# Residue-major token order, crossbar transposes for the last four batches and half-array transposes for the first, in a fused attention and feed-forward kernel

## Chip, cores, metric

One core of one Trainium2 chip. The metric is device time in microseconds (us). A profiled execution gives a *span*, some 1.7 us shorter than the run's time, and the mean clock granted to the matrix engine. The engines are PE (matrix), DVE (vector), ACT (scalar), POOL (its queue issues the casting loads from memory) and SP (its queue issues the stores and, after the change, the crossbar transposes). Tiles are counted from 0, so the second tile is tile 1.

## The reference, cut

```python
# q, k, v: (8 batches, 8 heads, 576 tokens, 64), drawn as randn * 0.1
scores = q @ k.T / 8
mask_plain = (rel >= 0) & (rel < 32)                       # heads 0..3
mask_dil   = (rel >= 0) & (rel < 128) & (rel % 4 == 0)     # heads 4..7
attn = softmax(where(mask, scores, -1e9)); out = attn @ v  # x: (4608, 512)
h = relu(x @ w_in); y = (h * h) @ w_out                    # 512 -> 2048 -> 512
```

## The kernel before

Heads go in pairs `e`; pairs 0 and 1 are plain, 2 and 3 dilated. Tokens of a dilated head are wanted by residue modulo 4. For each batch and pair: q and k (`qb`, `kb`) are transposed on PE into PSUM (`pa`), copied into `qT` and, block-diagonally, into `kbd`; scores, exponential and mask give `pt`; value products (`po`) and the denominator (`pd`, a product with ones) give a piece of `xT`. The feed-forward runs in nine tiles of 512 tokens. Each tile has `G` = 32 slots of four matmuls of 512 columns, and batch b's attention steps are mixed into tile b-1 at given slots.

```python
def t_main(b, e, nm):                       # batches 0, 2..7 (cut)
    for hl in range(2):
        for jp in range(4):                 # 8 transposes of 72 columns for q or k of a pair
            nc.tensor.transpose(pv_[:, hl, 72*pos : 72*pos+72], rbs[b][nm][0:72, 2*e+hl, 128*jp : 128*jp+128], ident[0:72, 0:72])
    for hl in range(2):
        for jj in range(2):                 # 4 copies of 64 x 288, or 4 + 4 for k of a dilated pair
            ...
            elif nm == "q":                 # plain: every second element of qT (4 bytes apart)
                nc.scalar.copy(qT[rows, e, :].rearrange("p (u a j) -> p j u a", a=4, j=2)[:, jj], ...)

def t_part(b, e, nm, part):                 # batch 1, in two parts of tokens (cut)
            elif nm == "q":                 # plain: every fourth element (8 bytes apart)
                nc.scalar.copy(qT[rows, e, ...].rearrange("p (x c j) -> p j c x", c=2, j=2)[:, jj], src)

# denominators of half a dilated pair: three wide matmuls
dms = [(d3[:, :, 0:96], main[:, :, 0:96]), (d3[:, :, 64:M], main[:, :, 96:176]), (d3[:, :, 128:M], rem)]
# store of 128 output rows: one DMA
nc.sync.dma_start(out[tk0 + P*m : tk0 + P*m + P, :], osb[:, :])
```

The softmax here doesn't subtract the row's maximum and nothing guards it: scores larger than these inputs give would overflow.

Of the kernel before, what the change touches and what calls it, by code (L numbers as in the profile page):

```python
# [11 lines left out]
WIN = 32  # L12
RES = 4

ORDER = (0, 2, 1, 3)

FIRST = "q0 k0 q3 q2 k2 a0 k1 b0 q1 v2 o0 a1 a2 k3 b1 o1 b2 p0 o2 p2 a3 v3 b3 p1 o3 p3".split()
# [3 lines left out]
        "21:q1 23:k0 24:q2 25:k2 26:q0 27:v2 27:v3 27:a0 27:a2 28:k1 28:k3 29:o0 29:a1 29:Q1 29:q3 29:o2 "  # L21
        "29:o1 30:a3 30:Q0 31:K1 31:o3 32:K0 32:Q2 34:Q3 36:b0 37:b1 37:K2 37:K3 37:V2 39:p0 39:b2 39:V3 "
# [3 lines left out]
        "8:q0 10:k0 12:a0 12:b0 13:k1 13:q1 14:v2 14:v3 14:o0 16:q2 17:p0 17:a1 17:k2 19:b1 19:o1 21:a2 22:q3 "  # L26
        "24:b2 24:o2 25:k3 26:p1 26:a3 26:b3 27:p2 29:o3 31:p3"
# [4 lines left out]
def _masks() -> np.ndarray:  # L32





    j = np.arange(64)[:, None]
    c = np.arange(96)[None, :]
    band = ((c - j >= 0) & (c - j < WIN)).astype(np.float32)  # L40
    kr, km = j % RES, j // RES
    cc = np.arange(64)[None, :]
    qr, qm = cc // 16, cc % 16
    rem = ((kr == qr) & (qm - km >= 0)).astype(np.float32)
    one = np.concatenate([band, rem], axis=1)
    p = np.arange(128)
    ident = (p[:, None] == p[None, :]).astype(np.float32)
    ones = (p[:, None] // 64 == p[None, :] // 64).astype(np.float32)
    return np.concatenate([np.concatenate([one, one], axis=0), ident, ones], axis=1).astype(ml_dtypes.bfloat16)
# [3 lines left out]
def kernel(  # L53
# [9 lines left out]
    nc = tc.nc  # L63
# [13 lines left out]
    PT = 72  # L77
    JT = S // PT
    TA = 256
    NT = 512  # L80
    NTILES = NTOK // NT
    KT = DM // P
    NF = DFF // P
    MT = NT // P
    M = S // RES

    const = ctx.enter_context(tc.tile_pool(name="const", bufs=1))
    rb_pool = ctx.enter_context(tc.tile_pool(name="rb", bufs=2))
# [15 lines left out]
    mk = const.tile([P, 160 + 2 * P], bf16, name="mk")  # L104
    ident = mk[:, 160 : 160 + P]
    ones = mk[:, 160 + P : 160 + 2 * P]
    mask_p = const.tile([P, NB * 96], bf16, name="mask_p")
    mask_d = const.tile([P, 2 * 176 + 64], bf16, name="mask_d")
    mask_t = const.tile([P, 4 * 64 + 4 * 112 + 64], bf16, name="mask_t")
# [6 lines left out]
    xT = const.tile([P, KT, NTOK], bf16, name="xT")  # L116
    qT = const.tile([P, NE, S], bf16, name="qT")
# [6 lines left out]
    rbs, vds = {}, {}  # L124

    def load_qk(b: int, es):
        if b not in rbs:
            rbs[b] = {
                "q": rb_pool.tile([80, H, JT * D], bf16, name="qb"),
                "k": rb_pool.tile([80, H, JT * D], bf16, name="kb"),  # L130
            }
        for es_ in ([e for e in es if e < NE // 2], [e for e in es if e >= NE // 2]):
            if not es_:
                continue
            hs = slice(2 * es_[0], 2 * es_[-1] + 2)
            for nm, src in (("q", q), ("k", k)):
                if es_[0] < NE // 2:
                    nc.gpsimd.dma_start(  # L138
                        rbs[b][nm][0:PT, hs, :], src[b, hs, :, :].rearrange("h (p j) d -> p h (j d)", j=JT)
                    )  # L140
                else:
                    nc.gpsimd.dma_start(
                        rbs[b][nm][0:PT, hs, :].rearrange("p h (a x) -> p (h a) x", a=2),
                        src[b, hs, :, :].rearrange("h (a p r) d -> p (h a) (r d)", a=2, r=RES),
                    )

    def load_v(b: int, es):
        dst = vbd[b % 2]
        if b not in vds:
            vds[b] = vd_pool.tile([P, NE // 2, 2, RES * D], bf16, name="vd")  # L150
        for e in es:
            for hl in range(2):
                rows = slice(64 * hl, 64 * hl + 64)
                h = 2 * e + hl
                if e < NE // 2:
                    nc.gpsimd.dma_start(  # L156
                        dst[rows, e, :, rows], v[b, h].rearrange("(i p) d -> p i d", p=64)
                    )
                else:
                    nc.gpsimd.dma_start(  # L160
                        vds[b][rows, e - NE // 2, :, :],
                        v[b, h, 0:512, :].rearrange("(m p r) d -> p m (r d)", p=64, r=RES),
                    )
        if es[-1] == NE - 1:
# [7 lines left out]
    def load_part(b: int, part: int):  # L172

        t0, t1 = (0, TA) if part == 0 else (TA, S)
        if part == 0:
            rbs[b] = {
                "q": rb_pool.tile([80, H, JT * D], bf16, name="qb"),
                "k": rb_pool.tile([80, H, JT * D], bf16, name="kb"),
            }
            vds[b] = vd_pool.tile([P, NE // 2, 2, RES * D], bf16, name="vd")  # L180
        for nm, src in (("q", q), ("k", k)):
            nc.gpsimd.dma_start(
                rbs[b][nm][0 : (t1 - t0) // 4, :, 256 * part : 256 * part + 256],
                src[b, :, t0:t1, :].rearrange("h (p j) d -> p h (j d)", j=4),
            )
        dst = vbd[b % 2]
        for e in range(NE):
            for hl in range(2):
                rows = slice(64 * hl, 64 * hl + 64)
                h = 2 * e + hl  # L190
                if e < NE // 2:
                    nc.gpsimd.dma_start(
                        dst[rows, e, t0 // 64 : t1 // 64, rows],
                        v[b, h, t0:t1, :].rearrange("(i p) d -> p i d", p=64),
                    )
                else:
                    nc.gpsimd.dma_start(
                        vds[b][rows, e - NE // 2, part, :],
                        v[b, h, t0 : t0 + TA, :].rearrange("(p r) d -> p (r d)", r=RES),
                    )  # L200
        if part == 1:
            for hl in range(2):
                rows = slice(64 * hl, 64 * hl + 64)
                nc.gpsimd.dma_start(
                    dst[rows, NE // 2 : NE, 8, rows],
                    v[b, H // 2 + hl : H : 2, 512:S, :].rearrange("h p d -> p h d"),
                )

    def spread_part(b: int, e: int, part: int):
        for hl in range(2):  # L210
            rows = slice(64 * hl, 64 * hl + 64)
            nc.vector.tensor_copy(
                vbd[b % 2][rows, e, RES * part : RES * part + RES, rows],
                vds[b][rows, e - NE // 2, part, :].rearrange("p (r d) -> p r d", d=D),
            )

    def spread_v(b: int, e: int):

        for hl in range(2):
            rows = slice(64 * hl, 64 * hl + 64)  # L220
            nc.vector.tensor_copy(  # L221
                vbd[b % 2][rows, e, 0:8, rows],
                vds[b][rows, e - NE // 2, :, :].rearrange("p m (r d) -> p (m r) d", d=D),
            )


    def t_main(b: int, e: int, nm: str, pool=None, name="pa"):



        ps = (pool or ps_a).tile([P, 1024], bf16, name=name)
        dil = e >= NE // 2
        pv_ = ps[:, 0 : 2 * S // 2].rearrange("p (h x) -> p h x", h=2)
        for hl in range(2):
            for jp in range(JT // 2):
                pos = 2 * (jp % 2) + jp // 2 if dil else jp
                nc.tensor.transpose(  # L237
                    pv_[:, hl, PT * pos : PT * pos + PT], rbs[b][nm][0:PT, 2 * e + hl, P * jp : P * jp + P], ident[0:PT, 0:PT]
                )
        for hl in range(2):  # L240
            rows = slice(64 * hl, 64 * hl + 64)
            for jj in range(2):
                src = pv_[64 * jj : 64 * jj + 64, hl, :]
                if dil:
                    src = src.rearrange("p (c m) -> p c m", c=2)
                    if nm == "q":
                        nc.vector.tensor_copy(  # L247
                            qT[rows, e, :].rearrange("p (c j m) -> p c j m", c=2, j=2)[:, :, jj, :], src
                        )
                    else:  # L250
                        nc.vector.tensor_copy(
                            kbd[rows, e, 0:8, rows].rearrange("p (m c j) k -> p c j m k", c=2, j=2)[:, :, jj, :, :],
                            src[:, :, 0:128].rearrange("p c (m k) -> p c m k", m=2),
                        )
                        nc.vector.tensor_copy(
                            kbd[rows, e, 8, rows].rearrange("p (m c j) -> p c j m", c=2, j=2)[:, :, jj, :],
                            src[:, :, 128:M],
                        )
                elif nm == "q":
                    nc.scalar.copy(  # L260
# [423 lines left out]
```

## Time and profile before

| | before |
|---|---|
| time, median (3 runs) | 342.56 us (342.47 to 345.79) |
| span of the profiled run | 341.6 us |
| PE busy, matmuls | 315.0 us, 2508 |
| first feed-forward matmul starts at | 27.61 us |
| period of a tile mixed with attention, from tile 2 on | 34.65 us |
| a tile without attention | 27.7 us |

PE is the engine to watch. A stage in which it hardly waits (the mixed tiles from the third on) can only be shortened by fewer or shorter matmuls; a stage in which it waits (up to 78 us) by whatever it waits for. The prediction below shows the lines. It calls PE *cold* near the start of the program and *warm* later: in the kernel before, eight 72-column transposes take 0.46 us from start to start at 13.38 us and 0.26 us at 206.86 us.

### The profile page before, as it was taken

Reading aid. Unit: us, or ns where it says so; the run is one execution under the profiler, and the core shown is the slowest. Engines: PE = TensorE matmul, PEld = TensorE weight load, DVE = VectorE, ACT = ScalarE, POOL = GpSimd, SP = SyncE. Lnnn points to the kernel's source line nnn. Section 1 sums busy time; section 2 is a strip of 40 time slices with the busy share of each in tenths; the row PEclk is TensorE's granted clock in tenths of the full one; section 3 lists DMA queues with packets and bytes.
Section 4 is the critical chain, followed back from the end, with each engine's and each line's share of the span. In section 5 each row is a group of like instructions: output and inputs, shape, how many; then the busy total and the mean of one; then the engine's idle time right before and its main releaser. Section 6 shows DMA issues by size and latency. Waiting matters only on the chain.

```text
span 341.6 us, 6597 instructions
## 1 busy us (share of the span) xinstructions
PE 315.0 (92%) x2508; PEld 182.6 (53%) x2508; DVE 205.6 (60%) x598; ACT 216.1 (63%) x449; POOL 87.2 (26%) x133
## 2 busy tenths in 40 slices
PE   1579998689999999999999999999999999999995
PEld 1464543475875555555556555555556555545542
DVE  6777518699895866486748674867376824302400
ACT  5385744859686794689468936893689447524611
POOL 8651387326126206500541044100000000000000
PEclk9999999999999999999999999999999999999999
DMA  7999999939429506920593049400100010011011
GB/s 93 128 190 215 179 147 144 139 62 145 92 38 159 76 2 100 182 52 2 89 174 71 2 78 171 85 0 34 61 34 2 31 63 32 0 63 61 0 61 61
DMA packets 52478, 28.32 MB, mean 83 GB/s; under 512 B 27168, under 2 KB 46816, under 8 KB 52448
## 3 DMA queue, kind: packets, MB, share of 16 engines
q0 software_dynamic: 47120, 18.37, 46.6%
q1 hardware_dynamic: 5184, 9.44, 7.6%
q8 instruction: 19, 0.31, 0.3%
q10 hardware_dynamic: 144, 0.11, 0.1%
q14 instruction: 11, 0.09, 0.1%
HBM read 36.81 MB, written 9.44 MB: 135 GB/s over the span
## 4 chain that ended last, share of the span: by engine, by line
PE 70%; ACT 10%; DVE 9%; DMA 6%; issue 3%; POOL 1%; ACTq 0%; DVEq 0%; POOLq 0%
PE pf L580 34%; PE pf L553 25%; PE pa L237 3%; DVE kbd L265 3%; ACT qT L260 3%; DMA kb<-in_k_dram 2%; ACT h2T L563 2%; PE po L482 2%; PE pd L482 2%; DMA qb<-in_q_dram 2%; DMA vd<-in_v_dram 2%; ACT qT L301 2%; PE pa L433 1%; ACT rec L485 1%; DVE h2T L564 1%
## 5 line engine op out<-in xcount | busy, mean ns | idle before, releaser
L553 PE MATMUL pf<-xT,w_in 128*128 128x512 bf16 (+1 forms) x640 | 136.8, 360 | 1.2 <-ACT osb L586 1.2
L580 PE MATMUL pf<-w_out_sb,h2T 128*128 128x512 bf16 x576 | 136.5, 379 | 0.0
L563 ACT ACTIVATE h2T<-pf 128x512 bf16<-128x512 f32 x144 | 82.6, 595 | 26.7 <-PE pf L553 25.2
L553 PEld LDWEIGHTS <-w_in 128*128 128x128 bf16 x640 | 67.7, 114 | 45.3 <-issue 3.7
L564 DVE TENSOR_TENSOR h2T<-h2T 128x512 bf16<-128x512 bf16 x144 | 58.0, 423 | 48.0 <-ACT h2T L563 46.6
L580 PEld LDWEIGHTS <-h2T 128*128 128x128 bf16 x576 | 51.8, 98 | 51.8
L586 ACT COPY osb<-pf 128x512 f32<-128x512 f32 x36 | 21.1, 586 | 41.8 <-PE pf L580 41.4
L484 ACT ACTIVATE rec<-pd 128x288 f32<-128x288 f32 (+2 forms) x52 | 21.5, 414 | 25.5 <-PE pd L482 23.6
L260 ACT COPY qT<-pa 64x288 bf16<-64x288 bf16 x56 | 26.7, 476 | 6.2 <-PE pa L237 5.7
L488 DVE TENSOR_TENSOR xT<-po,rec 128x288 bf16<-128x288 f32 x26 | 11.9, 458 | 28.3 <-ACT rec L485 28.1
L265 DVE COPY kbd<-pa 64x288 bf16<-64x288 bf16 x56 | 26.6, 476 | 2.1 <-PE pa L237 0.9
L439 ACT ACTIVATE pt<-pa 128x352 bf16<-128x352 f32 (+2 forms) x48 | 23.9, 502 | 4.6 <-PE pa L433 2.6
L485 ACT ACTIVATE rec<-rec 128x288 f32<-128x288 f32 (+2 forms) x56 | 24.8, 443 | 1.8
L482 PEld LDWEIGHTS <-vbd 128*128 128x128 bf16 x280 | 18.3, 103 | 12.8 <-issue 1.8
L138 POOL DMA_DIRECT2D qb<-in_q_dram x8 | 6.1, 766 | 70.7 <-PE pa L237 64.1
L160 POOL DMA_DIRECT2D vd<-in_v_dram x28 | 17.1, 619 | 23.8 <-DMA kb<-in_k_dram 12.0
L156 POOL DMA_DIRECT2D vbd<-in_v_dram x28 | 21.0, 764 | 3.1 <-DMA kb<-in_k_dram 2.7
L482 PE MATMUL po<-pt,vbd 128*128 128x96 bf16 (+1 forms) x260 | 18.6, 204 | 1.3 <-DVE vbd L221 0.5
L495 DVE TENSOR_TENSOR xT<-po,rec 128x320 bf16<-128x320 f32 (+1 forms) x26 | 12.0, 461 | 12.7 <-ACT rec L485 12.1
L237 PE MATMUL pa<-mk,qb 72*128 72x72 bf16 x224 | 12.6, 204 | 7.4 <-DMA qb<-in_q_dram 6.9
L247 DVE COPY qT<-pa 64x288 bf16<-64x288 bf16 x56 | 17.1, 305 | 3.2 <-PE pa L237 1.4
L482 PE MATMUL pd<-pt,mk 128*128 128x32 bf16 (+5 forms) x130 | 18.2, 239 | 0.0
(83 smaller groups left out, 283.2 us busy)
## 6 DMA issues: line engine op xcount, KB each, us to landing
out_dram<-osb SPq DMA_DIRECT2D x36, 256.0 KB, 3.0
qb<-in_q_dram POOLq DMA_DIRECT2D x13, 288.0 KB, 6.2
kb<-in_k_dram POOLq DMA_DIRECT2D x13, 288.0 KB, 8.0
w_out_sb<-in_moe_w_out_dram POOLq DMA_DIRECT2D x4, 512.0 KB, 16.9
vbd<-in_v_dram POOLq DMA_DIRECT2D x28, 72.0 KB, 8.9
vd<-in_v_dram POOLq DMA_DIRECT2D x28, 64.0 KB, 6.0
w_in<-in_moe_w_in_dram POOLq DMA_DIRECT2D x2, 512.0 KB, 7.0
w_in<-in_moe_w_in_dram POOLq DMA_DIRECT2D x1, 1024.0 KB, 12.4
```

The lines of the kernel that those rows point to most:

```text
L237: nc.tensor.transpose(pv_[:, hl, PT * pos : PT * pos + PT], rbs[b][nm][0:PT, 2 * e + hl, P * jp : P * jp + P], ident[0:PT, 0:PT])
L260: nc.scalar.copy(qT[rows, e, :].rearrange("p (u a j) -> p j u a", a=JT // 2, j=2)[:, jj, :, :], src.rearrange("p (a u) -> p u a", a=JT // 2),)
L265: nc.vector.tensor_copy(kbd[rows, e, :, rows].rearrange("p i (u a j) -> p j i u a", a=JT // 2, j=2)[:, jj, :, :, :], src.rearrange("p (a i ...
L439: nc.scalar.activation(pt[:, off : off + n], ps[:, 0:n], ACT.Exp, scale=SCALE)
L482: nc.tensor.matmul(oo, lh, rh, start=(x == 0), stop=(x == len(g) - 1), skip_group_check=True)
L484: nc.scalar.activation(rec[:, 0:n], d[:, 0:n], ACT.Ln)
L485: nc.scalar.activation(rec[:, 0:n], rec[:, 0:n], ACT.Exp, scale=-1.0)
L553: nc.tensor.matmul(acc[u][:, nt * x : nt * x + nt], w_in_sb[piece][:, kt, c0 : c0 + 509 : 4], xT[:, kt, tk0 : tk0 + nt], start=(kt == kts[ ...
L563: nc.scalar.activation(hv, acc[u][:, :].rearrange("p (x n) -> p x n", x=per), ACT.Relu)
L564: nc.vector.tensor_tensor(out=hv, in0=hv, in1=hv, op=ALU.mult)
L580: nc.tensor.matmul(cur[m][:, :], h2[:, f, P * m : P * m + P], w_out_sb[:, f, :], start=(f == 0), stop=(f == NF - 1),)
L586: nc.scalar.copy(osb[:, :], cur[m][:, :])
```

## The change

*Intent.* All tokens are kept in residue-major order, so q is copied densely and plain and dilated pairs share one code. The output rows then come out permuted, and stores put them back with a stride of four rows. q and k of batches 4 to 7 are transposed on the way from SBUF to SBUF by the DMA crossbar, a tile ahead, and PE no longer transposes them. The first batch's transposes use 64 columns of the array each, so that each head's data land on their own partitions and one wide copy of q replaces four (for k two replace four, or four replace eight). `xT` becomes a ring of four batches.

```diff
+    def cross(b, nm, part):                                   # batches 4..7, on the SP queue
+        nc.sync.dma_start_transpose(
+            (qx if nm == "q" else kx)[:, :, :, m0 : m0 + n].rearrange("p h c m -> p (h c) m"),
+            staged(b, nm)[0:n, part, :, :].rearrange("p h x -> p (h x)"))
+        if b == 0:                                            # 16 transposes on column halves
+            for r in range(RES):
+                for a in range(2):
+                    for hl in range(2):
+                        nc.tensor.transpose(pv_[64*hl : 64*hl+64, r, 72*a : 72*a+72],
+                                            t[0:72, 2*e+hl, a, D*r : D*r+D], ident[0:72, 0:72])
+            if nm == "q":
+                copy(qT[:, e, :, :], pv_)                     # one copy of 128 x 576
-        for g in (mms, [(a, ones[:, :], c) for a, c in dms]): # 2 or 3 wide denominators
+        for x, (i, oo, _, rh) in enumerate(mms):              # value products, block by block
+            nc.tensor.matmul(oo, vb[:, e, i, :], rh, ...)
+        for x, (i, _, dd, rh) in enumerate(mms):              # denominators, the same blocks
+            nc.tensor.matmul(dd, ones[:, :], rh, ...)
-                nc.sync.dma_start(out[tk0 + P * m : tk0 + P * m + P, :], osb[:, :])
+                store(osb, tk0 + P * m)                       # 1 to 3 DMAs, rows 4 apart
+        steps += attention_steps(b, G * (b - 1),              # b >= 4
+            {"k": (-9, 4), "q": (-9, 4), "v": (-7, 8), "a": (-1, 8), "b": (0, 8), "o": (3, 8), "p": (6, 8)})
+    CROSS = {4: 2 * G + 8, **{b: G * (b - 2) + 5 for b in range(5, B)}}
     (cut: loads in 1 KB rows for all heads, masks, ring, step orders of batches 0 to 2)
```

## The prediction

> **What bounds the kernel now.** I read the page first (busy shares, slices, chain), then busy time by stage, then the matrix engine (PE) in order of time inside one tile, then the groups with shapes kept apart.
>
> ```profile
> PE 315.0 (92%) x2508; PEld 182.6 (53%) x2508; DVE 205.6 (60%) x598; ACT 216.1 (63%) x449; POOL 87.2 (26%) x133
> PE   1579998689999999999999999999999999999995
> DMA  7999999939429506920593049400100010011011
> PE 70%; ACT 10%; DVE 9%; DMA 6%; issue 3%; POOL 1%; ACTq 0%; DVEq 0%; POOLq 0%
> ```
>
> PE is the bound: 92% busy and 70% of the chain that ended last. The idle tenths are all in the first quarter, where the DMA row is also at 9.
>
> The nine feed-forward tiles cut the run into stages. Batch b's attention is mixed into tile b-1, so tiles 7 and 8 have none. Columns: PE, weight load, DVE, ACT and POOL busy, clock, DMA share, GB/s.
>
> ```profile
> 28.00:65.37 37.37, 34.12 (x210) 16.51 (x209) 21.55 (x60) 21.55 (x46) 20.73 (x33) 1.00 1.22 171
> 65.37:109.00 43.63, 40.08 (x465) 30.36 (x462) 37.62 (x116) 32.74 (x72) 17.93 (x26) 1.00 0.72 90
> ...
> 178.30:213.00 34.70, 34.31 (x290) 19.58 (x289) 22.78 (x69) 24.71 (x53) 9.65 (x14) 1.00 0.59 83
> ...
> 309.95:337.65 27.70, 27.62 (x128) 13.29 (x126) 6.81 (x16) 11.90 (x20) 0.00 (x0) 1.00 0.10 38
> ```
>
> The chain of waits repeats with a period of 34.64 us (190.43, 225.08, 259.72) in tiles 2 to 6, while a bare tile takes 27.7 us. In that steady part PE waits only 0.39 us per tile, so a mixed tile is 27.7 us of feed-forward, some 6.5 us of attention matmuls and the wait. There, a matmul taken away is time taken away. The stages before are looser: some 13 us of the first 28 us and about 6.8 us of the next two stages are PE idle.
>
> **What the Trainium skill says.** "TensorE: Matmul & The Clock Gate", section "Wait — 56ns, not 53.3ns?": a warm matmul of N columns starts N / 2.4 GHz + about 2.5 ns after the one before, and never under about 25 ns. The trace agrees (start, span with the pipeline's tail, engine, line, tiles):
>
> ```profile
> 203.58 0.34 PE L482 MATMUL po<-pt,vbd 128*128 128x32 bf16 x5
> 203.76 0.33 PE L482 MATMUL pd<-pt,mk 128*128 128x256 bf16 x2
> 203.93 1.03 PE L580 MATMUL pf<-w_out_sb,h2T 128*128 128x512 bf16 x4
> ...
> 206.86 0.42 PE L237 MATMUL pa<-mk,qb 72*128 72x72 bf16 x8
> 207.12 1.89 PE L580 MATMUL pf<-w_out_sb,h2T 128*128 128x512 bf16 x8
> ```
>
> From start to start, eight 72-column transposes take 0.26 us, 32.5 ns each; the rule gives 32.5. The five value products (32, 96, 96, 96, 64 columns) take 0.18 us; the rule gives 25 + 3 x 42.5 + 29.2 = 182 ns. So PE can be counted by columns.
>
> "VectorE: DVE Perf Modes", section "What auto-detection actually checks": 16-bit operands of step 1 run at two elements a cycle, and at four when the one source and the destination are both in SBUF. The trace agrees:
>
> ```profile
> L265 DVE COPY kbd<-pa 64x288 bf16<-64x288 bf16 x8 | 3.8, 476 | 0.2
> L260 ACT COPY qT<-pa 64x288 bf16<-64x288 bf16 x8 | 3.8, 476 | 0.7 <-PE pa L237 0.7
> L247 DVE COPY qT<-pa 64x288 bf16<-64x288 bf16 x8 | 2.4, 305 | 0.3
> L221 DVE COPY vbd<-vd 64x512 bf16<-64x512 bf16 x4 | 1.2, 288 | 0.1
> L301 ACT COPY qT<-pa 64x128 bf16<-64x128 bf16 x8 | 3.5, 439 | 4.6 <-PE pa L277 4.6
> L307 DVE COPY kbd<-pa 64x128 bf16<-64x128 bf16 x8 | 3.5, 439 | 6.6 <-PE pa L277 6.4
> ```
>
> The same 288 elements cost 476 ns strided and 305 ns dense, and 512 from SBUF only 288 ns. With a fixed 155 ns (from the mask products, 338 ns for 352 elements and 406 ns for 480), that is 1.1, 0.52 and 0.26 ns per element. Line 301's and 307's writes, 8 bytes apart, cost 2.2.
>
> "DMA: Bandwidth & Descriptors", section "Latency and other measured facts", gives a crossbar transpose 261 GB/s. No trace of before has one.
>
> "TensorEngine Tiling (Array Packing)", "Feature Incompatibilities", says that column tiling excludes the fast weight load. No trace of before has that either.
>
> **The change, part by part.**
>
> *Crossbar for batches 4 to 7.* Removed: 64 transposes a batch, 64 x 32.5 ns = 2.08 us of PE. Added: small matmuls from the new cut. Every (head pair, part) now uses one list of blocks both for the value product and for the denominator, whereas before the denominator took two or three wide matmuls. The columns stay the same (3200 each for scores, values and denominators of a batch); the pieces grow by 10 score and 32 denominator matmuls. By the rule, before: 2.08 + scores 0.74 + 0.69, values 0.76 + 0.73, denominators 0.71 + 0.71 = 6.41 us. After: scores 0.76 + 0.78, values 0.76 + 0.78, denominators 0.76 + 0.78 = 4.62 us. PE: -1.79 us a batch. The tile's one wait, 0.39 us for strided copies out of PSUM that two buffers share with the scores, should mostly go too, since the copies now come eight or more slots ahead from SBUF. I take -2.0 us a tile, -8.0 in four.
>
> *Does anything take PE's place?* ACT loses the 3.8 us of line 260. DVE takes those copies over, but from SBUF: my estimate by the slopes above is 16 q copies at 230 ns, 8 k copies at 305, 8 at 222 and 8 at 200, in all 9.5 us against 10.3 now (3.8 + 2.4 + 2.3 + 1.8). DVE stays near 23 of 32.6 us.
>
> *The crossbar transfers* carry 2 x 8 x 576 x 64 x 2 bytes = 1.18 MB a batch, an estimated 4.5 us at the page's rate. They are issued at slot 5 of a tile and first read 18 slots later, each slot about 1 us. That leaves a factor of four.
>
> *Batches 2 and 3* keep transposes and get the extra matmuls: 4.62 + 2.08 - 6.41 = +0.29 us each. Batch 1 gets 30 extra denominator pieces (+0.17) and 80 rows instead of 64 in its first transposes (32 x 6.6 ns, +0.2). The ring cuts one tile's 64 matmuls in two, 64 x 2.5 ns = +0.16. Sum of these: +1.1.
>
> *First batch (to 28 us).* 128 half-width transposes replace 64, but one or two wide copies replace four or eight narrow ones. DVE: q of the dilated pairs 455 instead of 4 x 305 ns, k plain about 1.5 instead of 1.9 us, k dilated 1.3 instead of 2.0; that is 3.7 us less over the batch, and 2.5 us less on ACT. Half lies under the wait for loads (the last k of pairs 2, 3 arrives at 12.2 us), and PE, cold and busy there, gets some 100 more small instructions. Two zero fills of 16 x 2048 elements on ACT (an estimated 2 us each at 0.9 ns an element) delay the first q copy but should end before the load at 12.2 does. I take -1.5.
>
> *Batch 1 (43 to 78 us).* PE idles 5.5 us here behind lines 301 and 307. With q written densely and k at 4 instead of 8 bytes, the estimate is 155 + 0.9 x 128 = 270 ns against 439, and 296 against 439; for 160 elements 300 and 331 against 511 and 518. That takes 3.0 us off ACT and 2.6 off DVE in that chain, and the four strided products of line 399 (730 to 906 ns) fall to about 450, 1.5 us more. I take a bit under half as PE time: -2.3.
>
> *Tail.* The last store becomes two issues of about 0.33 us: +0.3.
>
> Sum: -8.0 + 1.1 - 1.5 - 2.3 + 0.3 = -10.4 us; 342.56 - 10.4 = 332.2, which I round to 332.5.
>
> **Rivals.**
>
> *A: the crossbar is slow and becomes the wait.* It writes runs of at most 160 bytes, all on the queue that also carries the stores, beside loads that already fill 0.6 of the 16 engines. For: packets are small, and no measured transpose exists here. Against: 18 us of lead against 4.5, and the queue has no stores until slot 19. If it took 25 us a batch, each of four tiles would lose some 5 us: 350.
>
> *B: the gain is only what the steady tiles give*, because early stages are bound by loads (DMA share 1.22 from 28 to 65 us) and cold matmuls. For: first-batch q, k loads of plain heads now move in 1 KB instead of 2 KB reads. Against: the first batch-1 transposes at 48 us come 6 us after their load landed, and PE then waits for lines 301 and 307. Time: 342.6 - 8.0 + 1.1 + 0.3 = 336, a change within 2%.
>
> *C: DVE's bursts become the wait.* k and q of a pair come at one slot, up to 12 copies or 2.7 us in a row. Against: products of the same slot are queued ahead of them, and values follow three slots after. If each burst held PE 0.3 us, 16 of them cost 5 us: 337.
>
> **Range and chances.** The steady gain is a count, good to about 1.5 us; the two early terms are each good to 2 us; A and C lengthen the slow side. I put 8 in 10 on 328.5 to 337. The 2% line is 335.7: B and C lie just beyond it, so 0.78 faster, 0.2 same, 0.02 slower.
>
> **What would show it.** Period of tiles 3 to 6: 32.4 to 32.8 us. Matmuls: 2508 + 196 = 2704. No PE wait on kbd in those tiles, ACT about 3.8 us lighter, DVE no heavier. Transposes landing within 10 us of issue. Feed-forward beginning near 26 us, and under 4 us of PE idle between there and the end of tile 1's first half. It would be wrong if the period stays above 33.5 us, if PE waits for qx or kx, or if the start grows beyond 28 us because the half-width transposes run one after another on a cold array.

## The result, and the profile after

| | before | after |
|---|---|---|
| time, median (4 runs each) | 343.28 us (342.47 to 345.79) | 331.94 us (331.05 to 332.49) |
| span | 341.6 | 330.3 |
| first feed-forward matmul | 27.61 | 26.38 |
| second tile begins | 65.37 | 61.51 |
| third tile begins | 109.08 | 105.47 |
| period of tiles 3 to 6 | 34.65 | 32.7 |
| matmuls | 2508 | 2704 |

The ratio is 0.9655, with a 95% interval of 0.9598 to 0.9713. Ratios in this document are the mean time of one kernel's fast runs over that of the other's of the same rounds, so not quite the ratio of the medians quoted.

The page of the kernel after, the same four lines:

```profile
PE 306.3 (93%) x2704; PEld 185.4 (56%) x2704; DVE 198.7 (60%) x608; ACT 199.1 (60%) x418; POOL 84.3 (26%) x129
PE   1579998989998999999999999999999999999994
DMA  6999999989967756999179927161210121031022
PE 75%; DVE 12%; ACT 6%; DMA 2%; issue 2%; POOL 1%; ACTq 0%; POOLq 0%
```

PE does 196 matmuls more in 8.7 us less, and is still the bound. DMA is fuller in the middle: the transposes. The stages after, in the same columns:

```profile
26.38:61.51 35.13, 33.58 (x225) 17.23 (x222) 19.74 (x56) 19.52 (x47) 17.73 (x27) 0.95 1.15 171
61.51:105.47 43.96, 40.47 (x531) 31.41 (x528) 35.21 (x116) 31.21 (x71) 19.28 (x28) 1.00 1.04 124
...
172.30:205.10 32.80, 32.62 (x335) 24.81 (x333) 23.33 (x77) 21.18 (x45) 9.38 (x15) 1.00 0.93 124
```

Against the stages before, the first became 2.6 us shorter, the second 0.25 us longer, and a late tile (the one that the ring cuts) 1.9 us shorter, with ACT lighter (24.71 to 21.18) and DVE heavier (22.78 to 23.33). The late denominators, counted from start to start as before:

```profile
138.03 0.44 PE L344 MATMUL po<-pt,vbd 128*128 128x32 bf16 x9
138.31 0.43 PE L346 MATMUL pd<-pt,mk 128*128 128x32 bf16 x9
138.58 1.02 PE L447 MATMUL pf<-w_out_sb,h2T 128*128 128x512 bf16 x4
```

The nine value products and the nine denominators of a dilated second part take 0.28 and 0.27 us; the column rule gives 4 x 25 + 4 x 35.8 + 29.2 = 272 ns. The one wait of PE in that tile, with the matmuls before it:

```profile
176.32 2.79 PE L419 MATMUL pf<-xT,w_in 128*128 128x256 bf16 x24
179.29 0.39 PE L344 MATMUL po<-pt,vbd 128*128 128x32 bf16 x6 [0.18 <-DVE xT L351]
```

The idle time in brackets is counted from the modelled end of the matmul before. From start to start the 24 matmuls take 2.97 us here and 2.63 us in experiment 2, where nothing waits, so this wait costs 0.34 us. In the same way the old wait of 0.39 us cost 0.56 (1.42 us from 194.82 to 196.24 for four matmuls that take 0.86 elsewhere). The copies (the last two lines are batch 1's):

```profile
L261 DVE COPY qT<-qx 64x288 bf16<-64x288 bf16 x17 | 4.3, 255 | 0.4
L265 DVE COPY kbd<-kx 64x288 bf16<-64x288 bf16 x8 | 3.8, 471 | 0.1
L272 DVE COPY kbd<-kx 64x256 bf16<-64x256 bf16 x8 | 1.8, 219 | 0.2
...
L265 DVE COPY kbd<-pa 64x128 bf16<-64x128 bf16 x8 | 2.4, 300 | 6.2 <-PE pa L248 6.1
L261 ACT COPY qT<-pa 64x128 bf16<-64x128 bf16 x8 | 2.1, 260 | 3.9 <-PE pa L248 3.9
```

The crossbar instructions of batch 5 on the SP queue, in order of time, and the first copy that reads them:

```profile
147.75 1.27 SPq L198 DMA_TRANSPOSE kx<-kb  x1
149.37 1.83 SPq L198 DMA_TRANSPOSE qx<-qb  x1
151.30 1.81 SPq L198 DMA_TRANSPOSE kx<-kb  x1
153.22 1.31 SPq L198 DMA_TRANSPOSE qx<-qb  x1
...
165.37 1.92 DVE L265 COPY kbd<-kx 64x288 bf16<-64x288 bf16 x4
```

Each holds the queue for 1.3 to 1.8 us. By the trace the last landed at 156.8 us, 9.1 us after the first began and 8.5 us before the first use. For the four batches this takes 8.4, 9.1, 9.6 and 9.0 us, and 8.1 us or more are left.

### The profile page after: what moved, and what is told of

Its sections match the earlier page's. It is cut to its first block, busy times and chain, and to the rows that moved or that the text cites. A ratio compares the mean times of both kernels' runs of the same rounds, so it can differ in the third digit from the quotient of the medians.

```text
span 330.3 us, 7043 instructions
## 1 busy us (share of the span) xinstructions
PE 306.3 (93%) x2704; PEld 185.4 (56%) x2704; DVE 198.7 (60%) x608; ACT 199.1 (60%) x418; POOL 84.3 (26%) x129
## 4 chain that ended last, share of the span: by engine, by line
PE 75%; DVE 12%; ACT 6%; DMA 2%; issue 2%; POOL 1%; ACTq 0%; POOLq 0%
PE pf L447 35%; PE pf L419 29%; DVE kbd L265 4%; PE po L344 3%; PE pd L346 3%; DMA kb<-in_k_dram 2%; DVE h2T L431 2%; DVE qT L261 2%; PE pa L311 1%; DVE pt L316 1%; ACT qT L261 1%; ACT osb L453 1%; ACT rec L348 1%; DVE xT L351 1%; PE pa L248 1%
## 5 line engine op out<-in xcount | busy, mean ns | idle before, releaser
L351 DVE TENSOR_TENSOR xT<-po,rec 128x256 bf16<-128x256 f32 (+1 forms) x56 | 25.4, 454 | 44.1 <-ACT rec L349 32.1
L348 ACT ACTIVATE rec<-pd 128x256 f32<-128x256 f32 (+1 forms) x56 | 23.0, 410 | 26.4 <-PE pd L346 26.3
L315 ACT ACTIVATE pt<-pa 128x352 bf16<-128x352 f32 (+3 forms) x56 | 27.9, 501 | 6.9 <-PE pa L305 6.5
L349 ACT ACTIVATE rec<-rec 128x256 f32<-128x256 f32 (+1 forms) x64 | 28.4, 444 | 2.0
L344 PE MATMUL po<-pt,vbd 128*128 128x96 bf16 (+3 forms) x315 | 20.0, 195 | 4.1 <-DVE xT L351 2.9
L346 PE MATMUL pd<-pt,mk 128*128 128x96 bf16 (+3 forms) x315 | 20.1, 196 | 0.0
L346 PEld LDWEIGHTS <-mk 128*128 128x128 bf16 x368 | 17.0, 99 | 0.6 <-issue 0.6
L265 DVE COPY kbd<-pa 64x288 bf16<-64x288 bf16 (+2 forms) x32 | 12.8, 399 | 6.7 <-PE pa L248 6.1
L261 DVE COPY qT<-qx 64x288 bf16<-64x288 bf16 x64 | 15.7, 245 | 1.4
L265 DVE COPY kbd<-kx 64x288 bf16<-64x288 bf16 x32 | 15.1, 471 | 0.3
```

Of the source, the lines that this page charges most:

```text
L265: copy(kbd[rows, e, m0 // 16 : (m0 + n) // 16, rows].rearrange("p i (m c j) -> p j i m c", c=2, j=2)[:, jj, :, :, :], src.rearrange("p c ( ...
L315: nc.scalar.activation(pt[:, off : off + n], ps[:, 0:n], ACT.Exp, scale=SCALE)
L344: nc.tensor.matmul(oo, vb[:, e, i, :], rh, start=(x == 0), stop=(x == len(mms) - 1), skip_group_check=True)
L346: nc.tensor.matmul(dd, ones[:, :], rh, start=(x == 0), stop=(x == len(mms) - 1), skip_group_check=True)
L348: nc.scalar.activation(rec[:, 0:n], d[:, 0:n], ACT.Ln)
L349: nc.scalar.activation(rec[:, 0:n], rec[:, 0:n], ACT.Exp, scale=-1.0)
```

## Experiments

Twelve kernels ran, all made from the changed kernel. Spans are of the profiled run; the changed kernel's is 330.3.

**1. Batches 4 to 7 back on PE.**

```diff
-    WHOLE = (0, 2, 3)
+    WHOLE = (0, 2, 3, 4, 5, 6, 7)
-        if what in "qk" and b >= 4:
+        if what in "qk" and b >= 99:
-    CROSS = {4: 2 * G + 8, ...}
+    CROSS = {}
-            {"k": (-9, 4), "q": (-9, 4), ...
+            {"q": (-7, 8), "k": (-5, 8), ...
```

> The changed kernel with the crossbar taken out: batches 4 to 7 loaded whole and transposed by PE like batches 2 and 3, everything else kept. Theory (the count by columns): each of four tiles gets 64 transposes of 32.5 ns back, +2.1 us, and the wait for strided copies out of PSUM, 0.2 to 0.4 us in place of the 0.2 us left now: the period of the late tiles goes from 32.7 to 34.7 to 35.0 us, the span from 330.3 to 338 to 339.5 us. Rival (the gain of the late tiles came from relief of PSUM and DVE rather than from PE work): the period goes above 35.5 us. Rival (the crossbar costs DMA and DVE time that eats part of the count): the period stays below 34.2 us.

Measured: span 342.0, median 342.98 us, ratio 0.998. This was above the expectation, and the fault was mine: the loads of batches 6 and 7 stood in program order before the last transposes of batches 4 and 5, whose buffers they take. PE waited 0.4 + 1.4 us in one tile and 2.1 us in the next for loads, and late pairs read the wrong batch. The comparison with the reference passed all the same, since scores of such small inputs give an almost even softmax. So this comparison says little about q and k in any kernel here, the changed one included. The two undisturbed tiles had periods of 34.48 us.

**2. The same, mended**, with `LOAD_QK` at `G*(b-3)+20` in place of `+6` for batches 6 and 7.

> The run without crossbar again, mended: in the first one the loads of batches 6 and 7 came in program order before the last transposes of the batches whose buffers they take, so PE waited on them (1.8 and 2.1 us in two tiles) and late pairs read the wrong batch; here they come after. Theory (the count): no wait on loads, all four late tiles at the 34.48 us that the two undisturbed ones of the first run had, 32.7 now; the span 330.3 + 4 x 1.8 + 0.3 = 337.8 us, 337 to 338.5. Rival (without the crossbar the loads cannot be placed so that PE does not wait): 340 or more.

Measured: span 337.3, median 339.32 us, ratio 0.9849 (0.9816 to 0.9882). A late tile of this run, and the place in it where the changed kernel waits:

```profile
174.44:209.03 34.59, 34.59 (x400) 26.79 (x396) 22.65 (x68) 23.95 (x53) 8.81 (x13) 1.00 0.58 83
```

```profile
179.00 2.79 PE L419 MATMUL pf<-xT,w_in 128*128 128x256 bf16 x24
181.63 0.39 PE L344 MATMUL po<-pt,vbd 128*128 128x32 bf16 x6
```

PE is busy through the whole tile, so without the crossbar there is no wait at all, and the crossbar's worth is the difference of the spans, 7.0 us for four batches, or 1.75 us each (64 x 32.5 ns = 2.08, less the wait of 0.34 us that the changed kernel has and this one has not, gives 1.74). It is PE work, counted as predicted. That the 0.39 us wait of before is gone here too shows that not the crossbar removed it but the new order of data and steps; this experiment does not part the two.

**3. The first batch's transposes at full width** (`if b == 0:` becomes `if b == 99:`, so the general path with narrow copies is taken).

> The changed kernel with the first batch's transposes at full array width (64 instead of 128, four or eight narrow copies instead of one or two wide ones). Theory: PE time of these transposes does not change, since the trace shows 16 half-width ones taking the 0.49 us that eight full ones took; what returns is copy time, about 2.5 us on ACT and 3.7 us on DVE, half of it hidden under the loads, so the feed-forward begins 1 to 2.5 us later than 26.4 us and the span is 331.3 to 333. Rival (the start is set by loads and by the new order of the steps): it begins within 0.5 us of 26.4.

Measured: span 333.8, median 335.53 us, ratio 0.9764. The feed-forward begins at 29.70 us, 3.3 us later; from there the run keeps the changed kernel's pace. That is more than expected: little of the saved copy time had been hidden under loads (DVE's copies for this batch take 6.5 us in the changed kernel and 10.0 here, and PE waits 2.26 us for one of them before the scores at 20.77 us). PE time is not the reason. Eight full-width transposes before, and sixteen half-width ones after, take 0.46 and 0.49 us from their start to the next instruction's:

```profile
13.38 0.66 PE L237 MATMUL pa<-mk,kb 72*128 72x72 bf16 x8
...
13.84 0.49 PE L433 MATMUL pf<-qT,kbd 128*128 128x96 bf16 x4
```

```profile
6.32 0.69 PE L214 MATMUL pa<-mk,kb 72*64 72x72 bf16 x16 [6.32 <-DMA kb<-in_k_dram]
6.81 0.68 PE L214 MATMUL pa<-mk,qb 72*64 72x72 bf16 x16
```

The two halves run side by side: the half-width transposes start in pairs 7 ns apart, a new pair every 60 ns, and the full-width ones every 60 ns one by one. What is saved is copies.

**4. Neither crossbar nor halves.** The first form carried the same faulty load schedule.

> Both taken out: only the residue-major token order, the row-strided stores, the unified blocks and the new order of the steps remain. Theory (the parts are additive): the span is that of the run without crossbar plus that of the run with full width less that of the changed kernel, about 339 to 342, so the order alone is worth 0 to 2.5 us against 341.6, being a gain of about 3 us in the second stage (26 to 62 us) and a loss of 0.3 us a tile later. Rival (the token order is the real source of the gain): the span stays below 337.

Measured: span 346.2, median 349.01 us; not used further. The mended form:

> The run with neither crossbar nor column halves, mended in the same way. Theory (additive): the mended run without crossbar plus the 3.3 us that full width cost, 340.5 to 342, about the time of the kernel before (341.6). Then token order, blocks and step order alone bring nothing net: what they save in the second stage is lost at the start, where the step order is made for wide copies. Rival: below 339, the order alone is a gain.

Measured: span 339.9, median 342.90 us, ratio 0.9953 (0.9920 to 0.9987). So the order alone, with blocks, stores and steps made for the other two parts, brings 1.7 us of span. By stage it starts the feed-forward 1.9 us later than before (29.55) and does the first tile in 34.35 us in place of 37.76; the second half of that tile takes 19.46 us, as in the changed kernel (19.47), against 22.45 before. This stage's gain belongs to the order. The four runs 339.9, 337.3 (with halves), 333.8 (with crossbar) and 330.3 (both) are additive within a microsecond: the halves give 2.6 or 3.5 us, the crossbar 6.1 or 7.0.

**5. Batch 1's plain copies done twice**, to test what PE waits for in batch 1's stage (42 to 62 us).

```diff
         halves(e, nm, pv_[:, :, :, 0:n], m0, n, copy)
+        if b == 1 and e < NE // 2:
+            halves(e, nm, pv_[:, :, :, 0:n], m0, n, copy)
```

> The changed kernel with each copy of batch 1's plain q and k out of PSUM done twice, which more than undoes the shortening of these copies (ACT +4.4 us, DVE +5.1 us against a saving of 3.1 and 2.6 us). Theory (PE in 43 to 78 us waits for these copies, so their shortening gave most of the 3.0 us that the second stage lost): the stage from the first to the second tile's start grows by 2.5 to 5 us, span 333 to 335. Rival (the 3 us came from elsewhere, the earlier loads or the new step order): the span stays within 1 us of 330.3.

Measured: span 336.8, median 338.84 us: 6.5 us longer, above the range. The first tile's second half grows by 4.7 us and the second tile by 2.7, and PE waits for just these copies:

```profile
54.85 0.32 PE L307 MATMUL pa<-qT,kbd 128*128 128x96 bf16 x4 [1.47 <-ACT qT L263]
59.09 0.33 PE L307 MATMUL pa<-qT,kbd 128*128 128x96 bf16 x4 [1.47 <-DVE kbd L267]
```

9.5 us of added copies cost 7.4 us in these two tiles, 0.8 us for each. The change took 5.8 us of copies away here, (439 - 260) x 8 + (511 - 285) x 8 ns on ACT and (439 - 300) x 8 + (518 - 338) x 8 ns on DVE. The stage became 3.0 us shorter. The copies are long enough to carry that; the doubling shows that the path runs through them, not that nothing else shared in it. In fact only 1.7 of the 3.0 us are less waiting (3.21 to 1.51 us); counted from start to start, the 64 feed-forward matmuls took some 0.8 us less and the transposes 0.5. Why these ran faster was not tested.

**6. Wide denominators in the new order.** The loop over blocks becomes 3 or 4 matmuls for a plain part and 1 or 3 for a dilated one. The dilated second part as an example:

```diff
-        for x, (i, _, dd, rh) in enumerate(mms):
-            nc.tensor.matmul(dd, ones[:, :], rh, ...)
+            pb = pt[:, c : c + 448].rearrange("p (r x) -> p r x", r=RES)
+            dms.append((d3[:, :, :], pb[:, :, 32:112]))
+            dms.append((d3[:, :, 0:32], pb[:, :, 0:32]))
+            dms.append((d3[:, :, 64:80], pt[:, c + 448 : c + 512].rearrange("p (r m) -> p r m", r=RES)))
+        for x, (dd, rh) in enumerate(dms):
+            nc.tensor.matmul(dd, ones[:, :], rh, ...)
```

> The changed kernel with the denominators in wide matmuls again (3 or 4 per plain part, 1 and 3 per dilated part, in place of 4, 6, 4 and 9), same columns, by access patterns of four dimensions in the new order. Theory (a matmul costs its columns plus 2.5 ns, never under 25 ns): 46 denominator matmuls a batch become 22, which saves 0.13 us a batch, of it 0.10 us in the dilated second parts, about 1.1 us in the whole; the period of the late tiles goes from 32.70 to 32.55 to 32.60 us. Rival (patterns with runs of 8 or 16 elements stream more slowly): the denominators of the plain pairs get longer than now and the period grows.

Measured: span 328.9, median 330.59 us, ratio 0.9627 (0.9587 to 0.9667); period 32.55 us in place of 32.70, the 0.13 us of the count. By the trace the tiles after that gain 0.7 us of the 1.4, less than the expected 1.1. The other 0.7 us is not the edit's: the first 64 feed-forward matmuls, which it does not touch, took 14.98 us in this run and 15.66 in the changed kernel's. The clock granted from 26 to 44 us was 0.94 and 0.91, but 1.00 in experiment 10's run, which took 15.54, so the clock alone does not explain it.

**7. Each crossbar transpose issued twice.**

```diff
                 for nm in "kq":
                     cross(b, nm, part)
+                    cross(b, nm, part)
```

> The changed kernel with each crossbar transpose issued twice, one after the other into the same place. Theory (hidden: four transposes a batch take about 8 us from issue to landing, 18 slots before the first use): 16 us a batch still fit; span 330.3 within 0.7 us, periods 32.7 within 0.2 us, DMA share up. Rival (crossbar or store queue near its limit): PE waits for qx, kx or a store, periods above 33.5 us, span above 333.

Measured: span 350.0, median 351.26 us, ratio 1.0214. My expectation fell. A repeat into the same place first waits for the earlier one to land, so eight took 24.6 to 31.6 us from first issue to last landing, not 16, and the last came after its first use. SP's queue, and PE:

```profile
150.10 6.11 SPq L198 DMA_TRANSPOSE kx<-kb  x2
156.38 4.65 SPq L198 DMA_TRANSPOSE qx<-qb  x2
161.12 5.66 SPq L198 DMA_TRANSPOSE kx<-kb  x2
166.88 7.88 SPq L198 DMA_TRANSPOSE qx<-qb  x2
```

```profile
178.78 0.59 PE L344 MATMUL po<-pt,vbd 128*128 128x32 bf16 x9 [5.41 <-DVE xT L351]
```

DVE stands before a copy that needs qx, the product behind it stands too, and PE waits for the PSUM that this product frees. So the form of the first rival is real: tiles 2 to 5 became 2.4, 7.5, 6.9 and 3.4 us longer, and the median of 351.3 us is near the 350 that the prediction's rival A gave for a crossbar of 25 us a batch. The test does not say what 16 us would cost.

**8. The transposes nine slots later in the program.**

```diff
-    CROSS = {4: 2 * G + 8, **{b: G * (b - 2) + 5 for b in range(5, B)}}
+    CROSS = {4: 2 * G + 14, **{b: G * (b - 2) + 14 for b in range(5, B)}}
```

> The changed kernel with the crossbar transposes issued nine slots later in each tile (slot 14 in place of 5, for batch 4 slot 14 in place of 8), so that some 9 us lie between issue and first use in place of 18. In the changed kernel's trace four transposes take about 8 to 10 us from first issue to last landing. Theory (the lead is about twice what is needed, and what hurt when each was issued twice was only that they came after their first use): this is the edge, PE waits at most 1 us a tile, span 330.3 to 334. Rival (transposes already cost something where they are, beside loads and stores): the span changes by the way the neighbours change, below 330, or above 335.

Measured: span 330.2, median 332.74 us. A miss of the experiment itself: the transposes began at the same time as before (147.67 us against 147.75). No store lies between the two places in SP's queue, and SP runs ahead of PE to its next wait, so a place in the program is not a time. How near the edge is stays with the trace: 8.5 us for batch 5.

**9. Plain q copies of batches 4 to 7 on ACT.**

```diff
-            halves(e, what, t[...], 0, M, nc.vector.tensor_copy)
+            halves(e, what, t[...], 0, M,
+                   nc.scalar.copy if what == "q" and e < NE // 2 else nc.vector.tensor_copy)
```

> The changed kernel with the plain pairs' q copies of batches 4 to 7 on ACT instead of DVE. Theory (the 0.18 to 0.24 us that PE still waits once a tile, for a product behind a burst of eight copies on DVE, is DVE's queue): the burst loses its four q copies, 1.0 us, the wait goes, the period goes from 32.70 to 32.45 to 32.55 us, the span to 329.3 to 329.7. Rival (ACT copies come in the way of the relu and the exponentials, and PE waits for those): no gain, or above 330.5.

Measured: span 329.6, median 331.34 us, ratio 0.9627; the last wait is gone and the period is 32.3 us. That is a little more than the expected 32.45 to 32.55, and fits the 0.34 us that the wait cost from start to start. The start was 0.4 us later and the first 64 feed-forward matmuls took 0.4 us longer, which the span still carries.

**10. Wide denominators and q on ACT together.**

> Wide denominators and q copies on ACT together. Theory (additive): 328.9 of the wide run less 0.8: 327.9 to 328.5. Rival (the two overlap): no better than 328.9.

Measured: span 328.6, median 330.38 us, ratio 0.9598 (0.9559 to 0.9637); period 32.2 us. The span is just above the expected 327.9 to 328.5. It is the fastest kernel by ratio and by period. Against the changed kernel the gain is about 0.5%; the two intervals against the kernel before overlap, and the periods (32.2 against 32.7 us, four tiles) are the better evidence.

**11. The same with batch 3 through the crossbar too** (`WHOLE = (0, 2)`, `CROSS[3] = G + 16`, `LOAD_QK[3] = G + 6`, steps in the pace of the later batches).

> The same, and batch 3 goes through the crossbar too: its loads come at slot 6 of tile 1 in place of 14, the transposes at slot 16, the copies in the pace of the later batches. Theory (the count): 64 transposes less, 2.1 us, if the loads land in time: 326 to 327 us. Rival (the second stage is short of load bandwidth, so the transposes wait on the sync queue for the loads and hold up the stores and the copies): 329 or more.

Measured: span 335.4, median 338.21 us. The rival's number was right. The transposes began at 83.4 us, each took 8.6 to 10.1 us from issue to landing (3.4 to 5.5 in the changed kernel), and the last landed 18.8 us after the first was issued. The DMA share there was 1.28. The copies waited for them, ACT the longest:

```profile
ACT qT L261 <- DMA qx<-qb: 8.9, 1, 8.9
```

```profile
105.84 0.56 PE L344 MATMUL po<-pt,vbd 128*128 128x32 bf16 x6 [9.15 <-DVE xT L370]
```

2.1 us of PE work was saved and 9.2 us of PE time lost to one late transfer, and the clock granted from 102.2 to 114.6 us was 0.69. The lead was short too, 7 slots in place of 18: ACT stood from 93.4 us, 10.0 us after the first issue, a lead that the 8.4 to 9.6 us of the changed kernel's batches would just have met. That the loads slowed the transposes is likely but was not tested, and neither was a longer lead.

## Why the prediction came out right, step by step

Terms of the sum against the traces; the trace's terms add up to the 11.3 us between the spans.

| term | predicted | measured |
|---|---|---|
| tiles 3 to 6 | -8.0 | -7.2 (137.86 to 130.70 us) |
| first batch, start of the feed-forward | -1.5 | -1.2 |
| first 64 feed-forward matmuls (15.31 to 15.66 us) | none | +0.35 |
| batch 1's stage | -2.3 | -3.0 (22.45 to 19.47 us) |
| extra matmuls in the second and third tile (and the ring, in tile 4) | +1.1 | +0.25, -1.0 |
| bare tiles | 0 | -0.1 |
| tail after the last matmul (4.0 to 4.6 us) | +0.3 | +0.6 |
| sum | -10.4 | -11.3 |

*The count by columns* held everywhere: for the transposes (experiment 2), for the small denominators (6), and for the ring's tile, 0.1 us longer than its neighbours (the count gave 0.16). The third tile came out shorter instead of longer because a quarter of batch 4's transposes used to lie in it, 16 x 32.5 ns = 0.5 us, which I had booked to the later ones, and because the wait of 0.39 us, which it had too (0.56 us from start to start), went. The prediction's "32 denominator matmuls" are 26 denominators and 6 value products; its sum has them right.

*The copies out of PSUM* were predicted to within 5%: 270 and 296 ns (measured 260 and 300), 300 and 331 (285 and 338), 455 for the dilated q (458). The strided products of batch 1, given as about 450 ns, took 424 and 492.

*Steps that were wrong or mis-sized.* First, "8 k copies at 305" from SBUF: they took 471 ns, the same as from PSUM; dense q copies took 255, near the 230. A tile's copies therefore took 11.3 us (16 x 255, 8 x 471, 8 x 219 and 8 x 202 ns), not "9.5 us against 10.3", and DVE got heavier. It did no harm beyond the new wait of 0.34 us a tile, because the copies come early; experiment 9 takes even that away. Second, the crossbar's time: "an estimated 4.5 us" was 8.4 to 9.6, so the lead was not "a factor of four" but under two. The conclusion survived, with less room than I claimed; experiments 7 and 11 show what the other side looks like. Third, the tile's 0.39 us wait was not removed by the crossbar (experiment 2); in its place the crossbar kernel has a new one, 0.34 us against 0.56 from start to start. Fourth, "half lies under the wait for loads" for the first batch: in experiment 3 the start came 3.3 us later for 3.5 us of DVE copies, so nearly all of them lay on the path. The predicted -1.5 was near by luck: two errors cancelled, since the new step order, without the wide copies, begins 1.9 us later than before (experiment 4). Fifth, the 5.5 us of PE idle time from 43 to 78 us were put down to lines 301 and 307; the waits that end there are 2.5 of 5.8 us, and the others end at copies of dilated k (0.7), exponentials (1.1) and a copy of output rows (1.2). The change cut the idle time of these stages to 2.7 us, so the -2.3 had the right cause among others.

*The signs.* The period, the matmul count, no wait on kbd, the start, landing within 10 us and little idle time before the second half of tile 1 (2.8 us) came out as listed; ACT became 3.5 us lighter; "DVE no heavier" did not.

*The rivals.* A (crossbar too slow) did not happen at this placement; experiments 7 and 11 produce it. B (only the steady tiles gain) is wrong: 3.9 us of the 11.3 came before 62 us. C (DVE bursts) is real at 0.34 us a tile, not at 0.3 us for each of four bursts.

## What to carry to other kernels

Where the matrix engine never waits, count columns: moving transposes to the crossbar was worth their matmul time (2.08 us a batch) less the wait that came with it (0.34 us), as long as they landed before their first use. A transfer that comes late can be worse than the work it replaced (9.2 us lost for 2.1 in experiment 11), since the engine stood at the copy and everything behind it stood too; judge the lead by issue and landing times of the trace, not by places in the program. And where the matrix engine waits on copies, the layout written counts: a microsecond of copies was worth 0.5 us (dense q in batch 1's stage) to 0.9 us (wide copies in the first batch).

## What the Trainium skill lacked or had wrong

- "DMA: Bandwidth & Descriptors", "Latency and other measured facts": the crossbar rate of 261 GB/s was not reached. Four SBUF to SBUF transposes of 64 or 80 rows, 1.18 MB, took 8.4 to 9.6 us from first issue to last landing beside ordinary loads, an estimated 123 to 140 GB/s, and each held the SP queue for 1.3 to 2.5 us.
- "SBUF — State Buffer", "Specifications (TRN2)": two hits in each 16-byte line are said to be enough for full bandwidth. Copies that wrote 2-byte elements 8 bytes apart, two to a line, took 439 ns for 128 and 518 ns for 160 on DVE, 300 and 338 at 4 bytes: an estimated 2.2 ns an element against 1.1, with 155 ns fixed (from 338 ns for 352 elements and 406 ns for 480). No run here changes the writes alone.
- "VectorE: DVE Perf Modes", "What auto-detection actually checks": my reading, that a strided copy from SBUF to SBUF would run at two elements a cycle, failed: 471 ns for 288 elements against 476 from PSUM. This is no error of the page: it asks for outermost dimensions that are even or equal, which the prediction left out, and these are 9 in the destination and may be merged otherwise in the source. No run tells whether that is the reason.
- "TensorEngine Tiling (Array Packing)", "Feature Incompatibilities", excludes the fast weight load with column tiling but gives no cost. In the first 27 us a weight load of 64 columns for the half-width transposes took 160 ns, one of 128 columns for the full-width ones in the kernel before 133 ns. The pace showed nothing of it: sixteen half-width transposes of 72 columns took 0.49 us, as eight full ones did (0.46 us).
